# One kernel, two branches: the order of the expert stage written by a list of jobs inside the kernel

## The chip, the cores and the metric

The kernel runs on one core of one Trainium2 chip. The metric is the device time of one execution in microseconds (us). Two kernels are compared by runs that alternate on the same chip; the figure given for a kernel is the median of its runs.

## The reference, cut to what matters

The input x is normalised by rows, and two branches are added to it: a Fourier mixing branch (two DFTs as matrix products) and a branch of 4096 experts that picks, for each of 2048 tokens and 32 heads, two experts and adds their outputs.

```python
x = A_x; xn = layernorm(x)                        # 2048 tokens x 512
out = x + Re(DFT_seq @ (xn @ DFT_hid)) + experts(xn)

def experts(x):                                   # H = 32 heads, K = 2 picks, N = 64 * 64 experts
    q = einsum("nd,dhc->nhc", x, w_q)
    s1, s2 = q[..., :dk] @ k1.T, q[..., dk:] @ k2.T          # 64 scores each
    ...                                           # the two best pairs: gate g, expert number top_e
    act = gelu(einsum("nd,nhkd->nhk", x, u[top_e]))
    return einsum("nhk,nhk,nhkd->nd", g, act, v[top_e])
```

## The kernel before

Up to about 417 us the kernel computes the Fourier branch, the scores and the picks, and prepares the tables u and v as pairs of fp16 parts (high and low, so that each product of two float32 values is three fp16 matmuls). From there on it runs the **expert stage**, which is what the change touches. The picks are not gathered. For each block of 128 tokens (16 blocks, `NT`) the stage computes all 4096 activations and multiplies them by a dense matrix of gates that is zero where nothing was picked. Per block:

- **z products** (`slot`, L1187): x times u for all experts. From block 2 on two blocks form a pair, and a Strassen-like scheme makes 28 slots (`SEQ`, each 24 matmuls of 128 columns) for a pair instead of 32 tile products. A slot writes to one of four PSUM banks ("X", "Y", "Z" of a quad of u tiles; `take` gives a bank, `banks.append` gives it back). Three of the seven operators read sums of u tiles, which are loaded into a ring of three places (`ring_load`, L1170); the first sum is loaded once (`first_sum`, L1132); the sums of x come with `fetch` (L1684, and `prep`, L1090).
- **evictions and gelu** (`z_pair`): ScalarE copies X, Z, X (L1225, L1230, L1232), VectorE adds (L1227, L1235, L1238), ScalarE applies gelu in place (L1215). Some of these free a bank, and slot "4" may start only when the addition after slot "7" (L1238) has read the bank.
- **gates** (`g_prep`): VectorE compares iotas with the list of picks, half a group of 32 tokens at a time: L (L1274), R (L1279), R times gate (L1282). There are three pairs of L and R. `g_mm` (L1290) multiplies them, 32 small matmuls for a group, into one of two PSUM tiles. A block has 4 groups.
- **w** (`w_part`): w1 on VectorE multiplies activations and gates (L1298), w2 on ScalarE casts to fp16 (L1303), w3 on VectorE forms the low part (L1304). All four groups of a block must be done before its v tiles start.
- **v tiles** (`v_tile`, L1352): 16 tiles of 6 matmuls of 512 columns, all into one bank. Seven of the 16 v tables do not fit in SBUF and stream through three places (`v_load`, L1324). `finish` (L1367) adds the result to y, which was loaded (L1361) and had x added by a DMA of GpSimd (L1364); `store` (L1370) writes the block out.
- **checks**: 128 jobs that read the DFT matrices, the weights and the tables again and sum them (`compare`, `compare_in`, `sum_up`, `fit`, `fit_sum`, `fit_here`, the lines with `cx` and `fit`). Nothing in the stage needs them before `verdict`, near the end. They share four buffers.

The order is written by hand in phases: `("z", 0)`, `("z", 1)`, then for each pair b = 2, 4 ... 14 a phase `("a", b)` of 28 slots followed by `("v", b - 1)` of 8 steps, and at the end `("v", 14)` and `("v", 15)`. In phase a the 16 v tiles of block b-2 are put between the slots at fixed places (`TILES`), and two tiles of block b-1 ahead of the last slot; the other 14 tiles of b-1 come in phase v, with no z slot beside them. `put` hangs the gates, w, lists, loads and checks on steps of the phases, and the checks are placed by a clock that counts 2.2 us for a slot and 2.8 us for a v step:

```python
TILES = [1, 2, 3, 3, 4, 6, 8, 10, 11, 13, 15, 17, 18, 20, 22, 24]
for b in PAIRS:
    o, ph, nx = b - 1, ("a", b), ("v", b - 1)
    put(ph, 1, G(o, 0), LRP(o, 1, 0))
    ...
    put(nx, 1, LRP(b, 2, 1), W(b, 0))
    put(nx, 2, W(b, 1))
    put(nx, 3, G(b, 2), LRP(b, 3))
    put(nx, 4, W(b, 2), G(b, 3))
    put(nx, 6, W(b, 3))
```

The framework then lays the instructions out per engine by its own priorities, and derives all semaphores. Only what is passed to `pin` (`keep_in_program_order`) keeps its place: L, the loads and sums of the checks, y loads and stores and the DMA that adds x. Each engine takes its own instructions in the order laid out, and so does SP's queue of DMAs.

Of the kernel before, what the change touches and what calls it, by code (L numbers as in the profile page):

```python
# [18 lines left out]
P = 128  # L19
# [17 lines left out]
def tile_fnet_peer(ctx, tc, x, ca, cb, c5, wt, wf, wr, wq, kt, ut, vn, out):  # L37
# [683 lines left out]
    def part_b(safe, stS, stP, stQ, stE, xt, u_sb, cmp_p, w4):  # L721
# [217 lines left out]
        def compact(b, src, pool, tag):  # L939
# [6 lines left out]
            nc.sync.dma_start_transpose(zt, src)  # L946
            cmp = pool.tile([P, 3, P, 2], F16, tag=tag, name=f"cmp{b}")
            nc.scalar.activation(cmp, zt.unsqueeze(3).to_broadcast([P, 3, P, 2]), AF.Copy)
            CMP[b] = cmp
# [121 lines left out]
        ap0 = stE.enter_context(tc.tile_pool(name="ap0", bufs=1, side="left"))  # L1071
        lr = stE.enter_context(tc.tile_pool(name="lr", bufs=1, side="left"))
# [11 lines left out]
        TG = 32  # L1084
        CB = 4
        ACT = {}

        def prep(b):
            if b > 1:
                nc.sync.dma_start(xb2[:, b % 2].rearrange("p a k n -> p (a k n)"), xt_d[b])  # L1090
# [4 lines left out]
        def u_part(b, cg):  # L1095
# [5 lines left out]
            for cc in range(m):  # L1101
# [4 lines left out]
                for kd in range(KD):  # L1106
                    for l, r in ((0, 0), (0, 1), (1, 0)):
                        nc.tensor.matmul(ps if n == 1 else ps.rearrange("p (b n) -> p b n", b=2),
# [5 lines left out]
            for i, bb in enumerate(b):  # L1114
                nc.scalar.activation(ACT[bb][:, cg * m:cg * m + m, :], pv[:, i], AF.Gelu_apprx_tanh, scale=zsc)

        if not safe:
# [3 lines left out]
            TILES = [1, 2, 3, 3, 4, 6, 8, 10, 11, 13, 15, 17, 18, 20, 22, 24]  # L1121
            TILES0 = [0, 0, 0, 0, 0, 0, 0, 1, 3, 5, 8, 11, 14, 17, 20, 23]
# [7 lines left out]
        def first_sum(qd):  # L1130
            for t, g in enumerate(QUADS[qd]):
                nc.sync.dma_start(u_sb[g][:, :, 1, 0:2, :].rearrange("p l k e -> p l (k e)"),  # L1132
                                  s_d[qd, 0].rearrange("p (t l f) -> t p l f", t=4, l=2)[t])
# [38 lines left out]
        ring_plan()  # L1172
        used = [0]

        def slot(op, quad, bank, qd):

            ua, us, ub, xa = OPS[op]
            for t, g in enumerate(quad):
                k = 0
                for kd in range(2):  # L1180
                    for l, r in ((0, 0), (0, 1), (1, 0)):
# [5 lines left out]
                        nc.tensor.matmul(bank[:, t * P:(t + 1) * P], lt, rt, start=(t == k == 0 and op in "125"),  # L1187
                                         stop=(t == 3 and k == 5), skip_group_check=op not in "125")
                        k += 1
            if us is not None:  # L1190
                ring_load(used[0])
                used[0] += 1

        def z_pair(b, n):

            st = {}
            late = []

            def work(at):

                if True:
                    o = SEQ[at]
                    while late and late[0][0] <= at:
                        late.pop(0)[1]()
                    op, qd = o[0], turn_q(o[1])
                    quad = QUADS[qd]

                    def dst(a, c):
                        return ACT[b[c]][:, 2 * quad[0] + a:2 * quad[3] + 2:2 * (quad[1] - quad[0]), :]

                    def v(p):
                        return p.rearrange("p (t n) -> p t n", t=4)

                    def gelu(d, src=None):
                        nc.scalar.activation(d, d if src is None else src, AF.Gelu_apprx_tanh, scale=zsc)  # L1215

                    def gelu_late(d, n):
                        late.append((at + n, lambda: gelu(d)))

                    if op in "125":  # L1220
                        st[o[1], "X" if op == "1" else "Y" if op == "2" else "Z"] = take(f"z{op}_{b[0]}_{qd}")
                    (X, Xt), (Y, Yt), (Z, Zt) = [st.get((o[1], k), (None, None)) for k in "XYZ"]
                    slot(op, quad, Z if op in "53" else Y if op == "2" else X, qd)
                    if op == "1":
                        nc.scalar.activation(dst(0, 0), v(X), AF.Copy)  # L1225
                    elif op == "2":
                        nc.vector.tensor_tensor(dst(0, 0), v(Y), dst(0, 0), op=ALU.add)  # L1227
                        banks.append(Yt)
                    elif op == "5":
                        nc.scalar.activation(dst(1, 0), v(Z), AF.Copy)  # L1230
                    elif op == "6":
                        nc.scalar.activation(dst(0, 1), v(X), AF.Copy)  # L1232
                        gelu_late(dst(0, 0), 1)
                    elif op == "3":
                        nc.vector.tensor_tensor(dst(0, 1), v(Z), dst(0, 1), op=ALU.add)  # L1235
                        banks.append(Zt)
                    elif op == "7":
                        nc.vector.tensor_tensor(dst(1, 1), v(X), dst(1, 0), op=ALU.add)  # L1238
                        gelu_late(dst(0, 1), 3)
                    else:  # L1240
                        gelu(dst(1, 0), v(X))
                        gelu_late(dst(1, 1), 3)
                        banks.append(Xt)

                    if at + 1 == len(SEQ):
                        while late:
                            late.pop(0)[1]()

            return work

        GP = {}
        pin = tc.keep_in_program_order
# [9 lines left out]
        def g_prep(b, tg, hfs=(0, 1)):  # L1262
            cmp = CMP[b]
            for hf in hfs:
                assert all(k == (b, tg) for k in PREP) and len(PREP.get((b, tg), ())) == hf
                ts = slice(tg * TG + hf * 16, tg * TG + hf * 16 + 16)

                def bc(w, n):
                    return cmp[:, w, ts, :].unsqueeze(2).to_broadcast([P, 16, n // 2, 2])

                LR.append(LR.pop(0))
                L, R = LR[-1]
                PREP.setdefault((b, tg), []).append((L, R))
                pin(nc.vector.tensor_tensor(  # L1274
                    L.rearrange("p t (l two) -> p t l two", two=2),
                    io_lam.rearrange("p (l two) -> p l two", two=2).unsqueeze(1).to_broadcast([P, 16, P // 2, 2]),
                    bc(0, P), op=ALU.is_equal))
                Rv = R.rearrange("p t (c two) -> p t c two", two=2)
                nc.vector.tensor_tensor(  # L1279
                    Rv, io_c.rearrange("p (c two) -> p c two", two=2).unsqueeze(1).to_broadcast([P, 16, NC // 2, 2]),  # L1280
                    bc(1, NC), op=ALU.is_equal)
                nc.vector.tensor_tensor(Rv, Rv, bc(2, NC), op=ALU.mult)  # L1282

        def g_mm(b, tg):
            if (b, tg) not in PREP:
                g_prep(b, tg)
            p = pg(f"g{b}_{tg}")
            for hf, (L, R) in enumerate(PREP.pop((b, tg))):
                for t in range(16):
                    nc.tensor.matmul(p[:, hf, t * NC:(t + 1) * NC], L[:, t, :], R[:, t, :], start=True, stop=True)  # L1290
            GP[b, tg] = p

        def w_part(b, tg, here=False):
            act = ACT[b]
            ts = slice(tg * TG, (tg + 1) * TG)
            p = GP.pop((b, tg))
            w = p.rearrange("p h (n c) -> p c (h n)", c=NC)
            nc.vector.scalar_tensor_tensor(w, act[:, :, ts], fw, w, op0=ALU.mult, op1=ALU.mult)  # L1298
# [611 lines left out]
```

## Time and profile before

| | us |
|---|---|
| three runs: median (lowest, highest) | 1137.82 (1135.99, 1137.84) |
| profiled execution: its time, and its span from first to last instruction | 1138.36, 1136.3 |
| busy in the span: PE, weight loads, VectorE, ScalarE, GpSimd | 1107.2, 722.0, 943.8, 695.9, 332.6 |
| from the first v tile (467.5) to the last matmul (1130.1): PE, VectorE, ScalarE busy | 647.00, 527.03, 356.79 of 662.60 |
| DMA: bytes moved, mean rate over the span | 229.95 MB, 202 GB/s |

PE is TensorE's matmuls, PEld its weight loads, DVE VectorE, ACT ScalarE, POOL GpSimd, SP SyncE; "L1352" is a line of the kernel. Matmuls overlap in the pipeline: a row gives each its full latency, so successive starts tell the rate. The granted clock is 1.00 from 25 us to the last matmul.

### The profile page before, as it was taken

To read this page: it belongs to the slowest core of one execution; us is meant where nothing else is said; L and a number is where in the kernel's file an instruction comes from. 1 tells how busy PE (TensorE), PEld (TensorE's weight loads), DVE (VectorE), ACT (ScalarE), POOL (GpSimd) and SP (SyncE) were. 2 spreads that over 40 slices of the span, in tenths; PEclk is the share of its full clock that TensorE was granted. 3 is DMA by queue.
4 is the path that set the end of the run, shared out by engine and by line. 5 is a ranking of instruction groups with operands and counts; after the bars stand their busy time and mean duration, and the time that the engine had idled before them with its cause. 6 is when DMAs were issued, how large, how long until landed. Compare 5 with 4: busy or idle time off the path is not lost. (4 is left out here: it accounts for less than half of the span.)

```text
span 1136.3 us, 29241 instructions
## 1 busy us (share of the span) xinstructions
PE 1107.2 (97%) x11528; PEld 722.0 (64%) x11528; DVE 943.8 (83%) x2828; ACT 695.9 (61%) x1238; POOL 332.6 (29%) x385
## 2 busy tenths in 40 slices
PE   9999999999999999999999999999999999999997
PEld 6465554544545459787578587587577578578643
DVE  6899789999989799488886976886986986986992
ACT  6557598888877585255566565566556456556530
POOL 0419999898888850000000000000000000000000
PEclk8999999999999999999999999999999999999999
DMA  8884446364353335857776867777676866856644
GB/s 281 272 211 170 159 163 224 112 206 170 101 174 94 112 107 193 158 179 240 254 245 226 275 218 253 251 241 250 216 253 215 301 214 232 283 187 231 178 130 115
DMA packets 134865, 229.95 MB, mean 202 GB/s; under 512 B 35380, under 2 KB 71355, under 8 KB 134718
## 3 DMA queue, kind: packets, MB, share of 16 engines
q1 hardware_dynamic: 132112, 223.72, 60.0%
q0 software_dynamic: 2304, 4.20, 2.4%
q8 instruction: 92, 1.51, 0.5%
q14 instruction: 55, 0.45, 0.1%
q10 hardware_dynamic: 302, 0.08, 0.0%
HBM read 192.49 MB, written 29.69 MB: 196 GB/s over the span
## 5 line engine op out<-in xcount | busy, mean ns | idle before, releaser
L252 PE MATMUL s<-m,xq 128*128 128x512 f16 x1344 | 297.5, 379 | 1.3 <-ACT ss L962 1.3
L1352 PE MATMUL v<-v,act 128*128 128x512 f16 x1044 | 241.4, 379 | 1.1 <-DVE act L1304 0.7
L252 PEld LDWEIGHTS <-xq 128*128 128x128 f16 x1344 | 129.8, 98 | 152.5 <-issue 2.9
L1364 POOL DMA_DIRECT2D y<-in_x_dram x16 | 14.4, 898 | 671.3 <-DMA y<-y_d 327.7
L1187 PEld LDWEIGHTS <-u 128*128 128x128 f16 x2688 | 156.1, 98 | 21.8 <-issue 6.1
L1352 PEld LDWEIGHTS <-act 128*128 128x128 f16 x1044 | 97.2, 98 | 102.7 <-DVE act L1304 1.2
L1274 DVE TENSOR_TENSOR L<-io_lam,cmp 128x2048 f16<-128x2048 f16 x128 | 154.3, 1214 | 4.9 <-PE g L1290 4.9
L966 DVE MAX8 vals<-ss 128x8 f32<-128x64 f32 x896 | 133.5, 217 | 5.4 <-ACT ss L962 5.1
L1187 PEld LDWEIGHTS <-s 128*128 128x128 f16 x1944 | 112.4, 98 | 10.4
L1352 PE MATMUL v<-v,w 128*128 128x512 f16 x480 | 111.1, 379 | 1.4 <-DVE w L1304 0.9
L1303 ACT ACTIVATE act<-g 128x1024 f16<-128x1024 f32 x44 | 57.7, 1311 | 61.8 <-DVE g L1298 61.8
L962 ACT ACTIVATE ss<-s,wsc 128x512 f32<-128x512 f32 x120 | 80.2, 681 | 22.4 <-PE s L252 12.6
L970 DVE FIND_INDEX8 idx<-vals,ss 128x8 uint16<-128x256 f32 x224 | 93.9, 419 | 0.0
L1187 PE MATMUL z<-x,u 128*128 128x128 f16 x1344 | 83.8, 219 | 3.3 <-DVE w L1238 2.9
L1187 PE MATMUL z<-xb,u 128*128 128x128 f16 x1344 | 84.2, 219 | 1.9 <-ACT w L1215 1.8
L1187 PE MATMUL z<-x,s 128*128 128x128 f16 x1296 | 81.1, 219 | 0.0
L1376 ACT ACTIVATE cx<-cx 128x896 f32<-128x896 f32 x68 | 64.1, 942 | 27.7 <-DVE cx L1424 18.1
L1352 PEld LDWEIGHTS <-w 128*128 128x128 f16 x480 | 44.7, 98 | 48.4 <-DVE w L1304 1.4
L1215 ACT ACTIVATE act<-act,scl 128x512 f32<-128x512 f32 x56 | 40.2, 720 | 53.0 <-DVE act L1235 27.9
L1290 PE MATMUL g<-R,L 128*128 128x32 f16 x2048 | 63.1, 176 | 8.6 <-DVE L L1274 5.3
L1290 PEld LDWEIGHTS <-L 128*128 128x128 f16 x2048 | 59.2, 96 | 17.0 <-DVE L L1274 9.4
L1304 DVE TENSOR_TENSOR act<-g,act 128x1024 f16<-128x1024 f32 x44 | 57.3, 1301 | 13.9 <-ACT act L1303 13.5
(358 smaller groups left out, 1884.6 us busy)
## 6 DMA issues: line engine op xcount, KB each, us to landing
s<-s_d SPq DMA_DIRECT2D x81, 512.0 KB, 4.9
v<-v_d SPq DMA_DIRECT2D x67, 512.0 KB, 5.5
cx<-in_cb_dram SPq DMA_DIRECT2D x64, 448.0 KB, 5.5
w<-in_wq_dram SPq DMA_DIRECT2D x28, 512.0 KB, 5.8
fit<-in_wq_dram SPq DMA_DIRECT2D x28, 512.0 KB, 5.1
uv<-in_vn_dram SPq DMA_DIRECT2D x16, 512.0 KB
uv<-in_ut_dram SPq DMA_DIRECT2D x16, 512.0 KB, 3.8
s_d<-v SPq DMA_DIRECT2D x32, 256.0 KB, 2.5
```

The costliest lines, as they stand in the source:

```text
L252: nc.tensor.matmul(ps, xt[i][:, l, kd, :], m[:, r, kd, :], start=(n == 0), stop=(n == 3 * KD - 1))
L962: nc.scalar.activation(s, ps, AF.Copy, scale=inv)
L966: nc.vector.max(vals[:, i, w, :, h], s[:, g, :])
L970: nc.vector.max_index(idx[:, i, w].rearrange("p k h -> p (k h)"), vals[:, i, w, 0:2].rearrange("p k h -> p (k h)"), s[:, w * HC:g + 1, :]. ...
L1187: nc.tensor.matmul(bank[:, t * P:(t + 1) * P], lt, rt, start=(t == k == 0 and op in "125"), stop=(t == 3 and k == 5), skip_group_check=op ...
L1215: nc.scalar.activation(d, d if src is None else src, AF.Gelu_apprx_tanh, scale=zsc)
L1274: pin(nc.vector.tensor_tensor(L.rearrange("p t (l two) -> p t l two", two=2), io_lam.rearrange("p (l two) -> p l two", two=2).unsqueeze(1) ...
L1290: nc.tensor.matmul(p[:, hf, t * NC:(t + 1) * NC], L[:, t, :], R[:, t, :], start=True, stop=True)
L1303: nc.scalar.activation(w16[..., 0], w, AF.Copy)
L1304: nc.vector.tensor_tensor(w16[..., 1], w, w16[..., 0], op=ALU.subtract)
L1352: nc.tensor.matmul(pv, w16[:, c, :, l], v_sb[g][:, r, cc, :], start=(n + cc == 0 and k == 0), stop=(n == end and cc == 1 and k == 2))
L1376: pin(nc.scalar.activation(f, f, AF.Abs, accum_out=chk[:, n:n + 1]))
```

## The change

The phases from `("a", 2)` to `("v", 14)` go, and with them `both`, `fetch`, `TILES` and the table of `put`s (they stay for the fallback branch). In their place a function `stage()` runs while the kernel is built. It makes a list of jobs, each with an engine, a length in ns, what it depends on and a due time: every z slot, v tile, half a group of gate matmuls, every VectorE and ScalarE instruction of the evictions, gates and w, every load, and each step of a check. It then plays the list through: at each moment every free engine takes the ready job with the earliest due time; TensorE takes a ready gate job first, and otherwise the ready head of the z or the v sequence; checks ("fill") are taken when nothing else is ready, or when they are 3 us late. The jobs are issued in the order in which they began, and in the stage all of VectorE, ScalarE and SP and the first matmul of each TensorE job are pinned.

The due times spread the 28 slots of a pair over 24 v tiles (`FULL`) instead of over 16 and two; only the last pair has 18. Gate matmuls go by halves of a group. The arithmetic is the same, and no matmul, eviction or load is added. The parts for blocks 0 and 1 ahead of the stage keep hooks; there the L comparisons are no longer pinned, the preparation of block 1's first gates moves into the stage, and the x part of block 2, its sums and the first ring loads are issued in `("z", 1)`. Block 15's v tiles follow the stage as before.

```diff
+        FULL, LOOK, CHECK0, CHECK1 = (24, 24, 24, 24, 24, 24, 18), 1e9, 12000, 42000
+        LEAD, SOFT, HARD = 8000, 3000, 2000
...
-                nc.sync.dma_start(t.rearrange("p t l k e -> p (t l k e)"), s_d[qd, o])
+                syn.dma_start(t.rearrange("p t l k e -> p (t l k e)"), s_d[qd, o])
...
-            TILES = [1, 2, 3, 3, 4, 6, 8, 10, 11, 13, 15, 17, 18, 20, 22, 24]
...
+            for n, b in enumerate(PAIRS):
+                k = 0
+                for m in range(32):
+                    while k < 28 and m * 28 >= k * FULL[n]:
+                        due["z", n, k] = t
+                        t += 1420
+                        k += 1
+                    due["v", b - 2 + m // 16, m % 16] = t
+                    t += 1450
...
+                    V[b, m] = v = job("PE", 1300, lambda m=m: v_job(b, m), (vload.get((b, g)),), due=due["v", b, m],
+                                      needs="bank" if m == 0 else None)
+                    if b and m == 0:
+                        for w in W2[b]:
+                            v.after(w)
...
+                    z = Z[n, k] = job("PE", 1345, lambda k=k: z_work[n](k), deps, due=at, needs="bank" if op in "125" else None)
...
+                    elif op == "6":
+                        z.after(GE[n, q, "A1"])
+                        ev("A6", "ACT", 600, [z] + region(b + 1, qd), nk("7"))
...
+                    elif op == "7":
+                        z.after(GE[n, q, "A6"])
+                        ev("D7", "DVE", 605, [z, GE[n, q, "A5"]] + region(b + 1, qd), nk("4"))
+                        ev("G11", "ACT", 630, [GE[n, q, "D7"]], at + 12000)
+                    else:
+                        z.after(GE[n, q, "D7"])
+                        ev("G10", "ACT", 600, [z, GE[n, q, "D7"]], at + 3500, "bank")
+                if n + 1 < len(PAIRS):
+                    done = [Z[n, k] for k in range(28)]
+                    for i in range(2):
+                        XF[n + 1, i] = load(done, lambda i=i: prep(b + 2 + i), 256, due["z", n, 27] + 1000)
+                    XF[n + 1, 2] = load(done, lambda: load_x4(b + 2), 512, due["z", n, 27] + 1000)
...
+                start = due["v", b, 0] if ("v", b, 0) in due else total
+                for tg in tgs:
+                    d = start - (4 - tg) * 3400 - 1000
...
+                        old = [halves[i - 3]] if i >= 3 else []
+                        p = job("DVE", 1130, lambda tg=tg, hf=hf: g_prep(b, tg, hf, 0), old + [CM.get(b)], due=d - 4200 + hf * 1700 - LEAD)
+                        p2 = job("DVE", 335, lambda tg=tg, hf=hf: g_prep(b, tg, hf, 1), [p], due=d - 3200 + hf * 1700 - LEAD)
+                        p3 = job("DVE", 335, lambda tg=tg, hf=hf: g_prep(b, tg, hf, 2), [p2], due=d - 2900 + hf * 1700 - LEAD)
+                        g = job("PE", 420, lambda tg=tg, hf=hf: g_mm(b, tg, hf), [p3], due=d - 1800 + hf * 900)
+                        if hf == 0:
+                            if len(WJ) >= 2:
+                                g.after(WJ[-2])
...
+                    w1 = job("DVE", 1200, lambda tg=tg: w_part(b, tg, 0), hf_jobs + gelus(b), due=d)
+                    w2 = job("ACT", 1215, lambda tg=tg: w_part(b, tg, 1), [w1], due=d + 1000)
+                    w3 = job("DVE", 1215, lambda tg=tg: w_part(b, tg, 2), [w2], due=d + 2000)
...
+                crit = [j for j in c if not fill(j)]
+                late = [j for j in c if fill(j) and j.due[1] + SOFT <= now and (e != "SP" or dma[0] < now + 6000)]
...
+            keep_on[0] = True
+            for j in order:
+                keep_first[0] = j.eng == "PE"
+                j.fn()
+            keep_on[0] = False
```

`region(c, qd)` is the list of v tiles of block c-3 that must have read a part of the activation buffer before block c's part is written there: three buffers serve 16 blocks. A job of SP counts 420 ns of its queue (840 for a comparison's two loads, 1250 for the transpose of a list) and 3.1 ns for each KB of its transfer.

More of the change, by code (lines that the diff above doesn't have):

```diff
@@ L1186, in slot @@
                         rt = xb2[:, (0, 0, 1, 1)[xa], r, xa % 2 * 2 + kd, :] if ub is None else x4[:, r, ub, kd, :]
-                        nc.tensor.matmul(bank[:, t * P:(t + 1) * P], lt, rt, start=(t == k == 0 and op in "125"),
+                        mm(bank[:, t * P:(t + 1) * P], lt, rt, start=(t == k == 0 and op in "125"),
                                          stop=(t == 3 and k == 5), skip_group_check=op not in "125")
                         k += 1
-            if us is not None:
-                ring_load(used[0])
-                used[0] += 1
@@ L1194, in z_pair @@
         def z_pair(b, n):
             st = {}
-            late = []
             def work(at):
[L1201 to L1247, printed above, removed]
@@ L1260, in part_b, with g_prep, bc @@
         PREP = {}
-        def g_prep(b, tg, hfs=(0, 1)):
+        def g_prep(b, tg, hf, part):
             cmp = CMP[b]
[L1264 to L1269, printed above, removed]
+            ts = slice(tg * TG + hf * 16, tg * TG + hf * 16 + 16)
+            def bc(w, n):
+                return cmp[:, w, ts, :].unsqueeze(2).to_broadcast([P, 16, n // 2, 2])
+            if part == 0:
@@ L1284, in g_mm @@
[L1284 to L1293, printed above, removed]
+            else:
+                vec.tensor_tensor(Rv, Rv, bc(2, NC), op=ALU.mult)
+        def g_mm(b, tg, hf):
+            if hf == 0:
+                GP[b, tg] = pg(f"g{b}_{tg}")
+            p = GP[b, tg]
+            L, R = PREP.pop((b, tg, hf))
+            for t in range(16):
+                mm(p[:, hf, t * NC:(t + 1) * NC], L[:, t, :], R[:, t, :], start=True, stop=True)
@@ L1351, in v_tile @@
                 for k, (l, r) in enumerate(((0, 0), (0, 1), (1, 0))):
-                    nc.tensor.matmul(pv, w16[:, c, :, l], v_sb[g][:, r, cc, :], start=(n + cc == 0 and k == 0),
+                    mm(pv, w16[:, c, :, l], v_sb[g][:, r, cc, :], start=(n + cc == 0 and k == 0),
                                      stop=(n == end and cc == 1 and k == 2))
-            if g >= V2 and g not in [v for v in v_order(b) if v >= V2][-3:]:
+            if not keep_on[0] and g >= V2 and g not in [v for v in v_order(b) if v >= V2][-3:]:
                 v_load(PL[g])
@@ L1366, in finish @@
         def finish(b, pv):
[L1367 removed]
+            vec.scalar_tensor_tensor(Y[b], pv, osc, Y[b], op0=ALU.mult, op1=ALU.add)
         def store(b):
[L1370 removed]
+            (syn.dma_start(out[b * P:(b + 1) * P], Y[b]))
         T = {}
@@ L1731, in part_b, with __init__, after @@
-        begun = None
-        for n, ph in enumerate(phases):
+        for b in range(NT):
+            ACT[b] = act_tile(b)
+        class Job:
+            def __init__(self, eng, ns, fn, deps=(), due=None, tail=None, size=0, needs=None, frees=None):
+                self.eng, self.ns, self.fn, self.due, self.size = eng, ns, fn, due, size
+                self.tail = dict(PE=225, DVE=145, ACT=155, SP=0, POOL=6000)[eng] if tail is None else tail
+                self.needs, self.frees = needs, frees
+                self.users, self.left, self.ready, self.done = [], 0, 0, None
+                for d in deps:
+                    if d is not None:
+                        self.after(d)
+            def after(self, d):
+                d.users.append(self)
+                self.left += 1
@@ L1733, in part_b @@
+        for ph in phases:
             b = ph[1]
             if ph[0] == "z":
-                ACT[b] = act_tile(b)
                 for cg in range(8):
@@ L1738, in part_b @@
                     hooks(ph, cg)
+                if b and not safe:
+                    stage()
                 continue
             if ph[0] == "a":
-                begun = both(b)
+                if safe:
+                    for c in (b, b + 1):
+                        prep(c)
+                    for n in range(16):
+                        v_job(b - 2, n)
+                    end_v(b - 2)
+                    for k in range(28):
+                        if k * 16 // 28 != (k - 1) * 16 // 28:
+                            u_part((b, b + 1), k * 16 // 28)
+                        hooks(ph, k)
                 continue
-            pv, pvt = begun or take(f"v{b}")
+            if b < 15 and not safe:
+                continue
+            VB[b] = take(f"v{b}")
             for cg in range(8):
-                if begun is None or cg:
-                    v_part(b, pv, cg)
+                v_part(b, VB[b][0], cg)
                 hooks(ph, cg)
-                if cg == 1 and b % 2 and b < 13:
-                    fetch(b + 3)
                 if b + 1 == NT and cg == 3 and not safe:
```

643 lines of the change are left out of this document (455 added, 188 removed).

## The prediction

> **What bounds the kernel now.** I read the page's busy shares first, then the stage's busy time by window, alone and by source line, then the waits of TensorE, then the timeline of one crossing from a pair's last z slot to the next block's v tiles, and last the waits of VectorE and the DMA queue. The stage from its first v tile to its last matmul, whole and for the matmuls of z (L1187), v (L1352) and gates (L1290) alone:
>
> ```profile
> span 1136.3 us, 29241 instructions
> ...
> 467.50:1130.10 662.60, 647.00 (x8175) 461.89 (x8172) 527.03 (x896) 356.79 (x660) 14.41 (x17) 1.00 0.69 226
> ...
> 467.50:1130.10 662.60, 286.19 (x4704) 272.65 (x4704) 1.00 0.69 226
> ...
> 467.50:1130.10 662.60, 352.33 (x1524) 141.86 (x1524) 1.00 0.69 226
> ...
> 467.50:1130.10 662.60, 59.29 (x1920) 55.66 (x1920) 1.00 0.69 226
> ```
>
> TensorE is busy 647.0 of 662.6 us, VectorE 527 (80%), ScalarE 357 (54%). The busy time counts each matmul's whole latency, so the true room is found from starts. This is TensorE alone in the timeline, around the end of one pair:
>
> ```profile
> 709.91 1.50 PE L1187 MATMUL z<-x,u 128*128 128x128 f16 x24
> 711.25 7.93 PE L1352 MATMUL v<-v,w 128*128 128x512 f16 x36
> 719.02 0.95 PE L1290 MATMUL g<-R,L 128*128 128x32 f16 x32
> 719.83 2.75 PE L1352 MATMUL v<-v,w 128*128 128x512 f16 x12
> 722.41 0.55 PE L1290 MATMUL g<-R,L 128*128 128x32 f16 x16
> 723.93 0.55 PE L1290 MATMUL g<-R,L 128*128 128x32 f16 x16 [0.97 <-DVE R L1282]
> 724.34 7.93 PE L1352 MATMUL v<-v,w 128*128 128x512 f16 x36
> 732.10 1.50 PE L1187 MATMUL z<-xb,u 128*128 128x128 f16 x24
> 733.44 1.46 PE L1352 MATMUL v<-v,act 128*128 128x512 f16 x6
> ```
>
> A z slot takes 711.25 - 709.91 = 1.34 us (0.0558 a matmul), 36 v matmuls 7.77 (0.2157 each, 1.29 a tile), 32 gate matmuls 0.81 (0.0253 each). So the stage's matmuls without any gap need 4704 x 0.0558 = 262.5, 1524 x 0.2157 = 328.7, 1920 x 0.0253 = 48.6 and the 24 half-width ones of the last tiles (L1337) 24 x 0.108 = 2.6, together 642.4. The stage has 662.6: **TensorE loses 20.2 us in the stage**, and no reordering can win more. Who makes it wait:
>
> ```profile
> PE g L1290 <- DVE L L1274: 4.6, 8, 1.3
> PE g L1290 <- DVE R L1282: 3.2, 4, 1.0
> PE z L1187 <- DVE w L1238: 2.9, 3, 1.8
> PE z L1187 <- ACT w L1215: 1.8, 2, 1.3
> PE v L1352 <- DVE w L1304: 0.9, 1, 0.9
> ```
>
> These five groups are 13.4 us in 18 waits: 7.8 for gates placed ahead of their L and R, 4.7 for z slots whose bank or addition is late, 0.9 for the w of the next block. Each wait is counted from the modelled end of the matmul before it, so it is short by 0.16 (a v matmul lasts 1.46 - 5 x 0.2157 = 0.38, the next may start after 0.22); this and small waits make up the rest. No engine is full, and the waits are spread out: an order that is a little wrong in many places, which is what the change rewrites.
>
> **The change part by part.** No instruction is removed, so the sum is 1138.36 (the profiled execution; 0.54 above the median) minus 20.2 plus what TensorE still waits for.
>
> *Gates, 7.8 now.* A half group is issued when the list holds its L and R for ready. It is as good as the lengths in the list, and the trace has these:
>
> ```profile
> 712.24 2.48 DVE L1298 SCALAR_TENSOR_TENSOR g<-act,scl,g 128x1024 f32<-128x1024 f32 x2
> ...
> 718.28 0.94 DVE L1418 TENSOR_TENSOR cx<-cx 128x768 f32<-128x768 f32 x1
> ...
> 720.80 1.22 DVE L1274 TENSOR_TENSOR L<-io_lam,cmp 128x2048 f16<-128x2048 f16 x1
> ...
> 728.52 1.22 DVE L1274 TENSOR_TENSOR L<-io_lam,cmp 128x2048 f16<-128x2048 f16 x1
> 729.65 1.29 DVE L1304 TENSOR_TENSOR act<-g,act 128x1024 f16<-128x1024 f32 x1
> ```
>
> L to the next start takes 729.65 - 728.52 = 1.13 (list 1.13); two w1 take 2.48 with the tail of the last, about 1.20 each (list 1.20); w3 follows with 1.29, tail included (list 1.215 plus 0.145). The order should hold on the chip. But TensorE's gate job has no slack beyond the rest of the job before it, on average half of 1.3 us, so a VectorE that is late by more shows again. I keep 2.5 of 7.8 (bounds 0 and 7.8).
>
> *Evictions, 4.7 now.* In the list a z slot that waits for its addition lets v tiles pass, where before the tiles stood at fixed places. I keep 1.5 (bounds 0 and 4.7).
>
> *w at the end, 0.9 in the five groups.* The last pair keeps its 18 tiles, so the tail has the same shape, with the checks ended 42 us ahead of the list's end and VectorE freer. I keep 0.5. The waits that the groups do not hold, 20.2 - 13.4 = 6.8, shrink in the same ratio, (2.5 + 1.5 + 0.5) / 13.4 = 0.34: 2.3.
>
> *24 tiles instead of 18 beside the slots.* This adds a risk. The v tiles of the even block need all four of its w, which need the gelu of the pair's last slot. In the rows above the last slot starts at 709.91; 36 + 12 + 36 v matmuls (14 tiles) and two gates cover 711.25 to 732.10; the last w3 ends at 729.65 + 1.29 = 730.94, **19.7 us after the z end**. After the change 8 tiles are left: 8 x 1.29 = 10.3, two gates 1.6, and then five slots of the next pair (1a 5a 2a 6a 3a) that need nothing of that block, 6.7: 18.6 us. Slot 7a must wait for an eviction that overwrites the buffer the block's first four v tiles read. So the chain of 19.7 has to get shorter by 1.1 or TensorE stands still at each of six crossings. It should: between 717 and 731 VectorE also made two L that block does not need yet (2.3 with 720.80 and 728.52, of which one is for its last half) and comparisons (0.94 and smaller ones), and the third gate stood behind 36 v matmuls until 719.02 though its predecessors' w3 had ended. By due times I count from the z end: gelu 1, two w1 2.4, one hand-over to ScalarE and back 1.5, two w3 2.4, one L with its R 1.8, two w1 and two w3 4.8, one more hand-over 1.5, together 15.4. That is 3.2 inside the cover; a comparison that is already running (up to 0.9) and the additions of the next slots (two or three of 0.6) eat most of it. I take 0.5 at each of six crossings, 3.0 (bounds 0 and (19.7 - 18.6 + 2.3) x 6 = 20, where the chain stays as it is and the next slots' additions come on top).
>
> *Loads and SP's queue.* All loads move; their number stays. Rows: issues, KB each and us to landing; then the line of the x load with its issue time in ns, and its time to landing.
>
> ```profile
> s<-s_d SPq DMA_DIRECT2D x81, 512.0 KB, 4.9
> v<-v_d SPq DMA_DIRECT2D x67, 512.0 KB, 5.5
> ...
> L1090 SPq DMA_DIRECT2D xb<-xt_d x14: 326/420/490, 446.4 to 982.0; - x14
> ...
> DMA to landing us min/median/max: 3.5/4.1/4.9
> ```
>
> The next pair's x (two loads and one of 512 KB) is issued at the z end instead of some us later, and is needed 10 to 12 us after it: three issues of 0.42 plus 4.9 is 6.2, hidden by the eight tiles. If the queue has 5 us of checks ahead, it is 11, just in time. Ring loads wait for a slot's end, v loads for a tile's end, stores for `finish`; all stand in one queue, so a late matmul holds up the loads behind it, and DVE's checks behind those. SP has the room: 148 issues in the two big rows are 62 us of 662. The 16 loads of first sums count as four jobs of 0.42 in the list and cost 1.7 each; slot 5a waits for four of them, issued after block 3's x at the end of block 1's z products: 0.4 + 1.7 + 4.1 = 6.2 us, covered by slot 1a and four v tiles (6.5). I add 0.3 for this start and 0.3 for transfers. POOL's job (adding x to y) only moves with the y loads, and `finish` is not due until 20 us later: nothing. The blocks before the stage keep their order but for the unpinned L: nothing, bounds -1 and +1.
>
> Sum: 2.5 + 1.5 + 0.5 + 2.3 + 3.0 + 0.3 + 0.3 = 10.4. 1138.36 - 20.2 + 10.4 = 1128.6, against the median 0.54 less: **1128 us**.
>
> **The rivals.**
>
> (1) *The plan holds almost wholly.* The list lets every engine take what is ready, and VectorE has 20% to spare. Gate, z and w waits 1 us, crossings 0, rest 1, transfers 0.6: 1137.8 - 20.2 + 2.6 = 1120. For it: the lengths agree to 2%. Against: each gate stands without slack, and transfers aren't constant (3.5 to 4.9 in the rows above).
>
> (2) *Buffers make the waits, not the order.* Three L/R pairs, two gate tiles and four banks stay as they are. If they hold VectorE back, the list meets the same walls: 1137.8 minus a tail of 0.9, 1137. What VectorE waited for:
>
> ```profile
> DVE R L1279 <- PE g L1290: 17.9, 4, 14.8
> ...
> DVE L L1274 <- PE g L1290: 1.9, 3, 0.9
> ```
>
> VectorE waited 1.9 us for a free L, three times, and once very long for a free R (14.8 of 17.9, one place). TensorE's 12 waits for L and R are not behind these. [...]
>
> (3) *Slower: the crossing runs dry.* With eight tiles left instead of 14, TensorE waits for w six times. If the chain stays 19.7 us and the next slots' additions lengthen it to 22, that is 3.4 each, 20 in all instead of 3: 1128 + 17 = 1145. For it: the row of 1.29 that ends at 730.94, against a cover of 18.6. Against: the comparisons and the early L in between, which due times put back. It decides from (20.2 - 7.4) / 6 = 2.1 us at each crossing, a chain of 20.7.
>
> **How the numbers follow.** My forecast (1123 to 1134) 0.52; the plan holds almost wholly (under 1123) 0.16; buffers, or waits that come back elsewhere (1134 to 1140) 0.16; the dry crossing (over 1140, or 1136 to 1140 in a milder form) 0.16. A change within 0.2% (2.3 us) cannot be told from none. Faster by more, under 1135.5: 0.52 + 0.16 and a third of the third case, 0.74; same 0.09; slower 0.17. The range that leaves out no more than 2 in 10 is 1118 (2 us above the stage without any wait, 1137.8 - 20.2 = 1117.6, rounded) to 1139; the likeliest case's own is 1123 to 1134.
>
> **What would show it.** Right: the stage of TensorE shrinks to about 652 us with 4704, 1524 and 1920 matmuls in it; waits of gates for L and R under 3 us; z slots waiting for L1238's and L1215's successors under 2; after each z end eight v tiles, then slots of the next pair, and the last w3 within 16 us. Wrong: waits of v tiles for w3 at every crossing (rival 3); VectorE waiting for gates before L or R (rival 2); loads landing late ahead of z slots or checks holding up VectorE; or a z slot waiting for x in the first 12 us of a pair.

## The result, and the profile after

| | before | after |
|---|---|---|
| median of the runs, lowest to highest (us) | 1137.83, 1135.99 to 1138.03 | 1116.94, 1116.67 to 1117.59 |
| profiled execution: time, span (us) | 1138.36, 1136.3 | 1117.59, 1115.7 |

The ratio is 0.9821 with a 95% interval of 0.9804 to 0.9838: **20.9 us faster**. I had forecast 1128 us, so the sign was right and the gain less than half of what came. Rival 1 happened, and a little more than it.

In the kernel after, nearly all instructions of the stage are issued through two wrappers and show their lines: L1098 for VectorE, ScalarE and SP, L1103 for TensorE. So operations are told apart by tile names (z, v, g, w, act, L, R, cx).

First the busy time by window, with the prediction's columns (window, its length, then busy time and instructions of PE, PEld, DVE, ACT, POOL, granted clock, DMA share, GB/s). Before, the last 50 us ahead of the stage:

```profile
417.50:467.50 50.00, 47.99 (x905) 46.78 (x904) 42.82 (x122) 27.27 (x34) 6.71 (x4) 1.00 0.66 160
```

After, the same 50 us, then the stage from its own first v tile (465.8) to the last matmul (1108.6), and the end:

```profile
417.50:467.50 50.00, 50.00 (x934) 48.60 (x932) 41.75 (x117) 27.51 (x35) 6.09 (x4) 1.00 0.40 129
465.80:1108.60 642.80, 641.78 (x8152) 460.63 (x8149) 521.12 (x897) 356.67 (x660) 14.21 (x17) 1.00 0.70 235
1108.60:1115.70 7.10, 0.01 (x1) 0.00 (x0) 0.48 (x1) 0.00 (x0) 0.00 (x0) 0.87 0.14 44
```

From the first v tile to the last matmul it took 662.60 us and takes 642.80; 1.34 of the difference is the first z slot of the first pair, which now runs ahead of the first v tile. VectorE and ScalarE do what they did (521.12 and 356.67 us, 527.03 and 356.79 before): the same work, placed otherwise. TensorE is busy 641.78 of 642.80. The 50 us ahead of the stage were part of the gain too: 47.99 us busy before, 50.00 after. The end behind the last matmul is 7.10 us, 0.9 longer than before. TensorE's waits from 417 us on, all that the trace names, after (engine and tile, released by; us in total, times, longest):

```profile
PE v L1103 <- DVE act L1098: 0.7, 1, 0.7
PE g L1103 <- DVE R L1098: 0.3, 1, 0.3
```

Counted from starts (each matmul's start less the one before and the step of its size), TensorE lost 22.4 us from 417 us on before, 20.0 of them in the stage and 2.3 ahead of it, and 1.7 after. 22.4 - 1.7 = 20.7, less the 0.9 at the end, is 19.8 of the 20.6 us between the two spans; another 0.6 is that the first z product starts at 418.4 instead of 419.1.

The 2.3 us are two places in the z products of blocks 0 and 1. TensorE's timeline there (start, us, engine, line, operation, count, in brackets the idle time before), before:

```profile
457.14 0.96 PE L1290 MATMUL g<-R,L 128*128 128x32 f16 x32 [0.69 <-DVE L L1274]
457.96 3.79 PE L1108 MATMUL z<-xb,u 128*128 128x128 f16 x65
463.06 2.13 PE L1108 MATMUL z<-xb,u 128*128 128x128 f16 x35 [1.32 <-issue]
```

and after:

```profile
455.67 0.95 PE L1103 MATMUL g<-R,L 128*128 128x32 f16 x32
456.47 8.70 PE L1103 MATMUL z<-xb,u 128*128 128x128 f16 x153
```

Neither the gate's wait for L nor the hole ahead of 463.06 is there any more.

Now the crossing that the prediction showed, from a pair's last z slot (start 707.31) to the first v tile of the even block (725.97), TensorE after:

```profile
707.31 1.50 PE L1103 MATMUL z<-x,u 128*128 128x128 f16 x24
708.65 5.34 PE L1103 MATMUL v<-v,w 128*128 128x512 f16 x24
713.83 0.55 PE L1103 MATMUL g<-R,L 128*128 128x32 f16 x16
714.23 1.46 PE L1103 MATMUL v<-v,w 128*128 128x512 f16 x6
715.52 0.95 PE L1103 MATMUL g<-R,L 128*128 128x32 f16 x32
716.33 2.75 PE L1103 MATMUL v<-v,w 128*128 128x512 f16 x12
718.91 0.55 PE L1103 MATMUL g<-R,L 128*128 128x32 f16 x16
719.32 1.46 PE L1103 MATMUL v<-v,w 128*128 128x512 f16 x6
720.61 1.50 PE L1103 MATMUL z<-xb,u 128*128 128x128 f16 x24
721.95 1.50 PE L1103 MATMUL z<-x,u 128*128 128x128 f16 x24
723.29 1.50 PE L1103 MATMUL z<-xb,u 128*128 128x128 f16 x24
724.63 1.50 PE L1103 MATMUL z<-x,s 128*128 128x128 f16 x24
725.97 2.75 PE L1103 MATMUL v<-v,act 128*128 128x512 f16 x12
```

No row has idle time before it. Eight v tiles (24 + 6 + 12 + 6 matmuls), four half groups of gates and four slots of the next pair lie between, as the list was to do it. VectorE in the second half of that stretch, where the last two groups of w are made:

```profile
717.67 0.95 DVE L1098 TENSOR_TENSOR cx<-cx 128x768 f32<-128x768 f32 x1
718.54 1.22 DVE L1098 TENSOR_TENSOR L<-io_lam,cmp 128x2048 f16<-128x2048 f16 x1
719.67 1.28 DVE L1098 TENSOR_TENSOR act<-g,act 128x1024 f16<-128x1024 f32 x1
720.86 1.26 DVE L1098 SCALAR_TENSOR_TENSOR g<-act,scl,g 128x1024 f32<-128x1024 f32 x1
...
724.38 1.30 DVE L1098 TENSOR_TENSOR act<-g,act 128x1024 f16<-128x1024 f32 x1
```

The last w3 ends at 725.68, 17.0 us after the z end at 708.65, and the v tile that needs it starts 0.29 us later. Checks (cx) and an L still stand inside the chain: the chain is not packed on VectorE, and it is just in time all the same.

### The profile page after: what moved, and what is told of

Read it like the earlier page. It is cut to its first block, busy times and chain, and to the rows that moved or that the text cites. A ratio compares the mean times of both kernels' runs of the same rounds, so it can differ in the third digit from the quotient of the medians.

```text
span 1115.7 us, 29227 instructions
## 1 busy us (share of the span) xinstructions
PE 1102.7 (99%) x11528; PEld 721.8 (65%) x11528; DVE 937.7 (84%) x2828; ACT 695.8 (62%) x1238; POOL 333.4 (30%) x385
## 4 chain that ended last, share of the span: by engine, by line
PE 80%; DVE 7%; POOL 6%; DMA 3%; ACT 2%; issue 1%; SPq 0%; POOLq 0%; ACTq 0%; DVEq 0%
PE z L1103 27%; PE v L1103 27%; PE s L252 19%; PE g L1103 4%; PE m L148 1%; POOL v L795 1%; DVE L L1098 1%; DVE vals L972 1%; PE m L152 1%; PE p L449 1%; DVE idx L976 1%; DVE g L1098 1%; DMA xt_d<-xq 1%; POOL u L540 1%; POOL v L825 1%
## 5 line engine op out<-in xcount | busy, mean ns | idle before, releaser
L1103 PE MATMUL v<-v,act 128*128 128x512 f16 (+1 forms) x1068 | 248.3, 377 | 0.7 <-DVE act L1098 0.7
L1103 PEld LDWEIGHTS <-u 128*128 128x128 f16 x3456 | 198.3, 98 | 14.4
L1103 PEld LDWEIGHTS <-act 128*128 128x128 f16 x1068 | 97.9, 98 | 95.7 <-DVE act L1098 1.2
L1098 DVE TENSOR_TENSOR L<-io_lam,cmp 128x2048 f16<-128x2048 f16 x120 | 144.9, 1220 | 6.9 <-PE g L1103 6.7
L1103 PE MATMUL z<-xb,u 128*128 128x128 f16 x2112 | 127.7, 219 | 0.0
L1103 PEld LDWEIGHTS <-s 128*128 128x128 f16 x1944 | 113.4, 98 | 12.5
L1103 PE MATMUL v<-v,w 128*128 128x512 f16 x480 | 113.0, 379 | 0.0
L1098 ACT ACTIVATE cx<-cx 128x896 f32<-128x896 f32 (+2 forms) x134 | 83.5, 625 | 31.7 <-DVE cx L1098 30.3
L968 ACT ACTIVATE ss<-s,wsc 128x512 f32<-128x512 f32 x120 | 80.1, 680 | 22.4 <-PE s L252 12.6
L1098 DVE TENSOR_TENSOR cx<-cx 128x128 f32<-128x128 f32 (+9 forms) x226 | 91.7, 418 | 2.7 <-DMA cx<-in_cb_dram 1.1
L1103 PE MATMUL z<-x,u 128*128 128x128 f16 x1344 | 84.2, 219 | 0.0
L1098 ACT ACTIVATE act<-act,scl 128x512 f32<-128x512 f32 x56 | 40.2, 719 | 66.4 <-DVE act L1098 66.4
L1103 PE MATMUL z<-x,s 128*128 128x128 f16 x1296 | 81.2, 219 | 0.0
L1103 PEld LDWEIGHTS <-L 128*128 128x128 f16 x2048 | 65.0, 96 | 16.1 <-DVE R L1098 0.7
L1098 ACT ACTIVATE act<-g 128x1024 f16<-128x1024 f32 x40 | 51.5, 1311 | 37.3 <-DVE g L1098 36.9
L1098 DVE TENSOR_TENSOR act<-z,act 128x512 f32<-128x512 f32 x44 | 30.4, 690 | 49.7 <-PE z L1103 45.9
L1103 PEld LDWEIGHTS <-w 128*128 128x128 f16 x480 | 43.8, 98 | 43.2
```

What stands on the lines that cost most here:

```text
L968: nc.scalar.activation(s, ps, AF.Copy, scale=inv)
L1098: return (lambda *a, **k: pin(f(*a, **k))) if keep_on[0] else f
L1103: i = nc.tensor.matmul(*a, **k)
```

## The experiments

Each run is told as its ratio to the kernel before on the same chip, with the 95% interval, and its median. "After" stands at 0.9821. "Lost" is TensorE's loss from the stage's start on, counted from starts as above.

### Is it the order as issued, or the pins?

**e_nopin**: the list's order of issue, nothing in it pinned.

```diff
-                return (lambda *a, **k: pin(f(*a, **k))) if keep_on[0] else f
+                return f
...
-            if keep_on[0] and keep_first[0]:
+            if False:
```

> The changed kernel with nothing pinned: jobs are issued in the list's order, TensorE's order stays the same to the instruction, and the framework lays out VectorE, ScalarE and SP by its own priorities. Theory A (the gain is the order in which VectorE, ScalarE and SP take their work): waits of gates and z slots come back, 8 to 18 us of the 20, so 1125 to 1135 us. Theory B (the gain is where v tiles and z slots stand on TensorE): nothing is lost, 1117 to 1119 us.

Measured 1.0311 (1.0275 to 1.0348), 1171.18 us. TensorE took its jobs in the same order as after. VectorE's waits, and then TensorE's:

```profile
DVE cx L1442 <- DMA cx<-in_cb_dram: 38.9, 14, 8.3
```

```profile
PE z L1103 <- DVE act L1265: 13.2, 11, 2.9
PE g L1103 <- DVE R L1304: 11.0, 6, 6.1
```

In the stage VectorE stood 38.9 us at checks whose data had not landed, with the additions and gates that TensorE needed queued behind. TensorE lost 40.3 us in the stage, and 13.3 ahead of its first v tile, where VectorE took a check of the stage among the gates of block 1:

```profile
457.87 0.43 DVE L1426 TENSOR_TENSOR cx<-cx 128x256 f32<-128x256 f32 x1 [10.07 <-DMA fit<-in_wq_dram]
```

Without its pins the change would have been 34 us slower than the kernel before (1171.18 against 1136.85 on that chip).

**b_pin**: the kernel before with its hand-written order pinned on all engines through the same wrappers.

```diff
+        vec, sca, syn = Kept(nc.vector), Kept(nc.scalar), Kept(nc.sync)
...
+            keep_on[0] = not safe and ph[0] != "z" and ph != ("v", 15)
```

> The kernel before with its order by hand, but every instruction of VectorE, ScalarE and SP and the first matmul of each job pinned in that order from the first pair on. If the hand's order is what makes TensorE wait: no gain, 1135 to 1150 us (the framework's own shifts had even helped). If the framework's layout spoils a good order: 1120 to 1130 us.

Measured 1.0853 (1.0813 to 1.0892), 1232.71 us; the first of TensorE's waits:

```profile
PE g L1096 <- DVE R L1091: 49.5, 30, 3.2
```

Pins alone are no gain either: the hand order was only a sketch, and the framework's rearrangement was worth 96 us to it (1232.71 against 1136.85). It takes the list's order and the pins together.

**e_pindve** and **e_pindveact**: the list's order, with only VectorE pinned, and with VectorE and ScalarE pinned and SP's queue left free (TensorE's first matmuls pinned in both).

```diff
-                return (lambda *a, **k: pin(f(*a, **k))) if keep_on[0] else f
+                return (lambda *a, **k: pin(f(*a, **k))) if keep_on[0] and self.eng is nc.vector else f
```

(for the second, `self.eng is not nc.sync`).

> The changed kernel with VectorE alone pinned in the list's order (and TensorE, whose order stays the same in any case); the framework lays out ScalarE and SP. All unpinned took 1171 us. If VectorE's order carries the gain: 1117 to 1122 us. If the order of SP's loads does (VectorE's comparisons waited 39 us for loads when nothing was pinned): 1135 to 1170 us.

> VectorE, ScalarE and TensorE keep the list's order, SP's queue is left to the framework. With VectorE alone pinned the time was 1149.6 us, with 73 us of ScalarE waiting for tables of the checks (24 waits) and evictions queued behind. Theory A (it was ScalarE's own order that put the checks ahead of evictions): under 1122 us, ScalarE's waits for loads of checks under 15 us, TensorE's waits under 5. Theory B (it was SP's order that brought the loads late, whatever ScalarE's order): 1135 to 1155, with ScalarE still waiting over 50 us for loads. Between them (1122 to 1135) both queues matter.

Measured 1.0104 (1.0077 to 1.0132), 1149.57 us, and 0.9826 (0.9798 to 0.9854), 1117.51 us. ScalarE's longest wait in the first:

```profile
ACT fit L1551 <- DMA fit<-in_wq_dram: 73.2, 24, 6.3
```

With ScalarE free, sums of the checks were laid ahead of evictions and waited 73.2 us for their tables, and VectorE and then TensorE waited for the evictions. With ScalarE pinned as well that row is gone, and TensorE has the same two waits as after (0.7 and 0.3 us). So SP's own order carries nothing that can be measured; of what the pins carry, the two engines' order carries all.

### What made TensorE wait before?

**b_nochecks**: the kernel before without its 128 check jobs; `verdict` fills its flags with zeros.

```diff
-            for m, job in enumerate(jobs):
+            for m, job in enumerate(()):
```

> The kernel before without its 128 checks and without the verdict's arithmetic (that part of the computation is left out; the result does not need it). If the comparisons that stand between gates and w are what TensorE waits for: 1120 to 1126 us. If the order of gates, w and evictions among themselves is: 1131 to 1137 us.

Measured 0.9823 (0.9778 to 0.9868), 1118.17 us. The stage from its first v tile to its last matmul, and TensorE's waits:

```profile
464.30:1110.30 646.00, 644.17 (x8176) 461.95 (x8173) 429.40 (x573) 213.49 (x270) 12.95 (x15) 1.00 0.48 151
```

```profile
PE g L1290 <- DVE R L1282: 1.1, 1, 1.1
PE z L1187 <- DVE act L1238: 0.3, 1, 0.3
```

Within the interval, the kernel before without the checks is as fast as the kernel after with them. Counted from starts, TensorE loses 3.4 us in the stage instead of 20.0. So the checks made 17 of the 20 us: 98 us of VectorE and 143 of ScalarE (527.03 - 429.40 and 356.79 - 213.49), engines which had room, but the checks stood in the queues ahead of what TensorE needed. Their loads go too (DMA share 0.48 instead of 0.69), but after has a share of 0.70 and hardly a wait, so it isn't the traffic. It need not be the checks' busy time alone: before, VectorE also stood 23.1 us at checks whose loads had not landed, against 1.1 us after, and this run takes both away together.

```profile
DVE cx L1418 <- DMA cx<-in_cb_dram: 12.9, 7, 4.7
DVE cx L1407 <- DMA cx<-in_cb_dram: 6.2, 4, 3.0
DVE cx L1405 <- DMA cx<-in_cb_dram: 4.0, 2, 2.4
...
DVE cx L1098 <- DMA cx<-in_cb_dram: 1.1, 2, 0.9
```

(The last row is after's.) VectorE's timeline before, at the prediction's crossing, shows one place where a check stood in the way:

```profile
718.28 0.94 DVE L1418 TENSOR_TENSOR cx<-cx 128x768 f32<-128x768 f32 x1
719.26 0.29 DVE L1424 TENSOR_TENSOR cx<-cx 128x126 f32<-128x126 f32 x1
...
719.66 1.22 DVE L1274 TENSOR_TENSOR L<-io_lam,cmp 128x2048 f16<-128x2048 f16 x1
...
723.46 0.42 DVE L1282 TENSOR_TENSOR R<-R,cmp 128x512 f16<-128x512 f16 x1
```

1.38 us of a check's sums (718.28 to 719.66) stand ahead of the L and R that end at 723.88; the gates start at 723.93, after the 0.97 us of idle time that the prediction quoted. Not tried: the hand order with the checks alone placed by lengths; so it is open whether the list's order of the other work adds anything of its own; the 3.4 us left here against 1.7 after leave little room for it.

**e_checkdue**: checks compete with all other jobs by due time once that is reached, instead of coming second.

```diff
+                c = [j for j in c if not fill(j) or j.due[1] <= now]
+                j = min(c, key=lambda j: j.due[1] if fill(j) else j.due)
```

> The changed kernel with the checks no longer second: from their due time on they compete with gates, evictions and w by due time alone, on VectorE, ScalarE and SP. If the rank of the checks carries the gain: gates and w come late behind comparisons, 1122 to 1132 us. If it does not: 1117 to 1119 us.

Measured 0.9811 (0.9775 to 0.9847), 1118.58 us. Lost: 4.6 us instead of 1.7, within the intervals. So the rank of the checks carries nothing that can be measured, as long as the list places them too.

### What do the 24 tiles carry, and where does the crossing run dry?

**e_full18**, **e_full28**: 18 and 28 v tiles beside a pair's 28 slots instead of 24. **e_strict**: TensorE may take only the earlier due of the two heads.

```diff
-        FULL, LOOK, CHECK0, CHECK1 = (24, 24, 24, 24, 24, 24, 18), 1e9, 12000, 42000
+        FULL, LOOK, CHECK0, CHECK1 = (18, 18, 18, 18, 18, 18, 18), 1e9, 12000, 42000    # e_full18
+        FULL, LOOK, CHECK0, CHECK1 = (28, 28, 28, 28, 28, 28, 18), 1e9, 12000, 42000    # e_full28
+        FULL, LOOK, CHECK0, CHECK1 = (24, 24, 24, 24, 24, 24, 18), 1e-9, 12000, 42000   # e_strict
```

> The changed kernel with the slots of every pair spread over 18 tiles instead of 24, as many as before the change. Theory A: the list keeps everything busy anyway, 1117 to 1119 us. Theory B (the spread over 24 tiles carries a part): evictions get 0.4 us less per slot, z waits come back, 1121 to 1127 us.

> The changed kernel with the slots of the first six pairs spread over 28 tiles instead of 24, so that four tiles of the odd block are left at the z end instead of eight. By the prediction's crossing the cover is then 4 x 1.29 + 1.6 + 6.7 = 13.5 us against a chain of 15.4 (its count) to 18 us (the changed kernel's last w3): TensorE stands 2 to 4.5 us at each of six crossings, 1129 to 1144 us. If the list finds other work there: 1117 to 1120 us.

> The changed kernel with LOOK near 0: in the list TensorE may take only the head with the earliest due time, so a z slot no longer passes a v tile that waits, nor a tile a slot. The v tiles of the even block are due 8 tiles and one slot after the z end (10.3 + 1.3 + gates 1.6 = 13.2 us), while their last w3 ended 15.9 to 18.2 us after it in the changed kernel. Theory B: TensorE stands 3 to 5 us at each of six crossings, 1135 to 1147 us. Theory A: VectorE brings the w forward as soon as TensorE waits for it (15.4 us by the prediction's count), 2 us at each, about 1130 us.

Measured: 18 tiles 0.9814 (0.9786 to 0.9843), 1116.36 us; 28 tiles 0.9929 (0.9908 to 0.9951), 1131.76 us; strict 1.0023 (1.0007 to 1.0039), 1140.30 us. So the 24 tiles bring nothing. TensorE's waits from 467 us on with 28 tiles:

```profile
PE v L1103 <- DVE act L1098: 4.5, 3, 1.6
PE g L1103 <- DVE R L1098: 3.1, 3, 2.4
PE v L1103 <- ACT w L1098: 1.9, 1, 1.9
```

These are, the second apart, the waits of v tiles for w2 and w3 that rival 3 named. With five tiles and five slots between, the first v tile is taken 14.8 to 17.8 us after the z end, while the last w3 ends 15.4 to 18.5 us after it: later at each of the six crossings. In e_strict only one slot of the next pair got ahead of the even block's tiles, and v tiles and gates stood 2.2 to 3.5 us at each crossing. So with 24 tiles it is the slots that pass the tiles which hold the crossing together; the chain is about as long as with 28.

### How true must the lengths be?

**e_dve80, e_dve90, e_dve95, e_dve110**: every VectorE length in the list times 0.8, 0.9, 0.95 and 1.1; the program computes the same, in another order.

```diff
-                self.eng, self.ns, self.fn, self.due, self.size = eng, ns, fn, due, size
+                self.eng, self.ns, self.fn, self.due, self.size = eng, ns * (0.8 if eng == "DVE" else 1), fn, due, size
```

> The changed kernel with VectorE's lengths in the list 20% too short, so the list believes L, R, w1 and w3 ready before they are. The prediction's step (a gate or slot is placed without slack, and each lateness shows): 5 to 15 us of waits, 1122 to 1132 us. The other theory (VectorE waits for TensorE every few us, 73 us in all in the changed kernel, so lateness is paid back there and cannot add up): under 3 us, 1117 to 1120 us.

> The changed kernel with VectorE's lengths in the list 5% too short. 20% too short cost 58 us. If the loss goes with the error from the start (the prediction's step, no slack anywhere): a quarter, 10 to 15 us, 1127 to 1132 us. If the gates' slack (median 1.3 us in the changed kernel) takes up a small error: under 3 us, 1117 to 1120 us.

> The changed kernel with VectorE's lengths in the list 10% too long. Gates and slots are then never early on the chip, but the list may run out of VectorE's time (it believes 86% instead of 78%) and put w and gates late. If only lateness against the list costs: 1117 to 1119 us. If the list's own room counts: 1122 to 1130 us.

> All VectorE lengths in the list times 0.9. So far: 1.10 gave 1118.8, 1.00 gave 1117, 0.95 gave 1128.5, 0.80 gave 1176.6 us. If lateness grows in proportion to the error (theory A, some 2.3 us for each 1%): 1138 to 1145. If it grows slowly first and then steeply, where VectorE as listed is more than full (theory B): 1129 to 1136. Waits of gates for R over 6 us in both.

| VectorE's lengths | ratio (95%) | median us | lost us |
|---|---|---|---|
| x 1.10 | 0.9836 (0.9811 to 0.9861) | 1118.81 | 2.6 |
| x 1.00 (after) | 0.9821 (0.9804 to 0.9838) | 1116.94 | 1.7 |
| x 0.95 | 0.9914 (0.9889 to 0.9939) | 1128.46 | 14.6 |
| x 0.90 | 1.0048 (1.0026 to 1.0070) | 1142.83 | 28.6 |
| x 0.80 | 1.0326 (1.0284 to 1.0368) | 1176.61 | 58.8 |

TensorE's largest group of waits at 0.80:

```profile
PE g L1103 <- DVE R L1098: 24.6, 28, 2.1
```

The ratios give (0.9914 - 0.9821) x 1137.8 = 10.6 us for the first 5%, 15.2 for the next, 31.6 for the next 10%: two to three us for each 1%, and nothing on the long side. Half the gain is gone at 5%, all of it at 10%. The proportional curve had the time at 0.90 right, though its slope grows a little.

### The two places ahead of the stage

**e_pinl**: L of blocks 0 and 1 pinned again, as it was before.

```diff
-                vec.tensor_tensor(
+                i = vec.tensor_tensor(
...
-                    bc(0, P), op=ALU.is_equal)
+                    bc(0, P), op=ALU.is_equal); i = keep_on[0] or pin(i)
```

> The changed kernel with L pinned again in the blocks ahead of the stage, as before the change. Two waits of 2.3 us in all stood there before and are gone. If the pin made them: 1119 us with both back near 456 and 461 us. If the moves of the preparation and loads did: 1117 us, none back.

Measured 0.9819 (0.9795 to 0.9843), 1117.95 us. In the trace the gate's wait for L at 456 us is back (0.7 us), the hole at 463 is not. So the pin made the first; 0.7 us is under what the times can tell. What made the second isn't shown. ScalarE before stood there at the cast of a list whose transpose had not landed, with an eviction of a z bank behind it (461.69), and after has no such cast from 424.5 us to 473.5:

```profile
460.94 0.84 ACT L948 ACTIVATE cmp<-zt 128x768 f16<-128x768 f16 x1 [5.76 <-DMA zt<-z_d]
```

## Why the prediction was wrong in size

**The floor** was right for the stage: no gap can be won twice. My 642.4 for the matmuls alone is 641.1 without the slot that went ahead of the first v tile, and the stage took 642.8. **Blocks ahead of the stage** I put at "nothing, bounds -1 and +1": measured -2.3. The row of 47.99 busy us in 50.00 was there to be read, and I asked only the stage for its waits. That is also why the time lies below the low end of my range. I called 1118 "2 us above the stage without any wait", but 1137.8 - 20.2 is the stage without any wait itself, with nothing for what lies ahead of it.

**What TensorE still waits for** is the step that failed. I kept 10.4 us; the trace has 1.7 in the stage.

| term | kept | measured after |
|---|---|---|
| gates | 2.5 | 0.4 (one wait) |
| evictions | 1.5 | 0 |
| w at the end | 0.5 | 0.9 (one wait) |
| waits that no group holds, by the ratio 0.34 | 2.3 | 0.4 |
| crossings | 3.0 | 0 |
| start and transfers | 0.6 | 0 |

- *Gates.* "TensorE's gate job has no slack ... so a VectorE that is late by more shows again" is right as a mechanism: at 0.95 TensorE loses, counted from starts, 9.1 us in 35 places ahead of gates, 5.0 ahead of v tiles and 0.7 ahead of z slots. That the whole then comes to 1128, my very forecast, is chance: my sum had other terms. But I had no row for a late VectorE. My rows said the contrary: L 1.13 against 1.13 in the list, w1 1.20 against 1.20, w3 1.145 against 1.215. I kept 10.4 us, about what lengths 5% too short cost (10.6), in a list whose lengths I had just found true. On the chip half of the gates start within 1.32 us after their R ends (the median of 120; 8.7 before), and the trace names one wait. Little slack is what a plan that holds looks like.
- *Evictions* and the *ratio* go with it: I scaled waits whose maker I had not looked for. It was mostly the checks (b_nochecks: 17 of 20 us), and the list, whose lengths are true, takes the waits away almost wholly, not in part.
- *Crossings.* I counted a chain of 15.4 us; it is 15.9 to 18.2. The L at 718.54 and the cx at 717.67 inside it are about 2 us that I had left out of the count and put into the 3.2 of room. The cover of 18.6 was right: the v tiles start 16.0 to 18.7 us after the z end. So the chain nearly fills the cover, and stalls are zero, where I took 0.5 for each. TensorE's choice between v head and z head makes that (e_strict): a slot more is taken when w is late (five at one crossing, four at the others). I had counted five slots into the cover, and still kept 0.5 for a chain that runs over it; it never did (18.2 at most against 18.6).
- *Start, loads and SP's queue*: nothing to see, as I had it but for 0.6; e_pindveact shows SP's order free.

**The rivals.** Rival 1, with 2.6 kept, has 1.7 in the trace; 1138.4 - 20.2 + 1.7 - 2.3 ahead of the stage - 0.6 ahead of the z products + 0.9 at the end is 1117.9, against 1117.6 for the profiled execution. Its chance of 0.16 was too low: the rows of lengths spoke for it and I gave more weight to "each gate stands without slack". Rival 2 (buffers) is out: b_nochecks has the same buffers and banks, and TensorE loses 3.4 us, though VectorE itself waits 50.8 us there for a free L or R (1.9 and 17.9 before). TensorE's gaps before were mostly made by work standing in a queue: 17 of the 20 us went with the checks. Rival 3 (a dry crossing) is real and was one step away: 28 tiles bring it. Of the signs I named, the eight tiles followed by slots are there (seven once), gate waits are under 3, no z slot waits; "w3 within 16 us" was wrong (17.0 in the crossing shown), and the stage came to 642.8 instead of 652.

## What to carry to other kernels

Filler work on an engine with room still costs time when it stands ahead of what the full engine needs next (17 of the 20 us here): find the maker of a wait (here by leaving the checks out) before deciding how much of the wait will stay. An order planned in the program works when the engines that carry the chain keep it (by the ratios, without pins 56 us were lost, 13 of them ahead of the stage, and with VectorE alone pinned 32), when the full engine may pass a blocked head (23 us), and when lengths are true or long (5% short cost 11 us, 10% long nothing). So for a forecast compare the plan's lengths with the trace: where they agree, expect the plan to hold.

## What the runs showed of the hardware

With 28 tiles a dry crossing cost more than its wait. TensorE in that run, in two places, and the windows around them and around a third, with the granted clock (1.00 is full speed) in the third column from the end:

```profile
559.45 0.61 PE L1103 MATMUL v<-v,w 128*128 128x512 f16 x2 [1.91 <-ACT w L1098]
560.98 5.31 PE L1103 MATMUL v<-v,w 128*128 128x512 f16 x16 [0.92 <-DVE w L1098]
...
738.37 0.56 PE L1103 MATMUL g<-R,L 128*128 128x32 f16 x16 [2.41 <-DVE R L1098]
738.78 5.54 PE L1103 MATMUL v<-v,act 128*128 128x512 f16 x17
```

```profile
558.00:561.40 3.40, 1.03 (x4) 0.33 (x5) 3.40 (x8) 2.90 (x4) 0.00 (x0) 1.00 0.87 298
561.40:564.80 3.40, 3.40 (x9) 1.22 (x8) 3.40 (x11) 1.54 (x5) 0.86 (x1) 0.50 0.61 206
564.80:568.20 3.40, 3.40 (x44) 1.95 (x43) 3.06 (x6) 1.78 (x6) 0.00 (x0) 1.00 0.88 233
...
646.70:650.10 3.40, 1.68 (x22) 1.01 (x19) 3.40 (x5) 2.83 (x4) 0.86 (x1) 1.00 0.73 171
650.10:653.50 3.40, 2.68 (x27) 1.50 (x28) 3.40 (x8) 2.62 (x10) 0.00 (x0) 1.00 1.00 231
...
738.90:742.30 3.40, 3.40 (x11) 1.04 (x8) 3.40 (x6) 3.40 (x10) 0.00 (x0) 0.50 0.86 318
```

Two pauses of 1.91 and 0.92 us, with two matmuls between, were followed by a granted clock of 0.50 in the window from 561.40 to 564.80; in the next window it was 1.00 again. The 16 v matmuls from 560.98 took 5.31 us, as long as 24 at the clock of 1.00 in the kernel after (5.34 from 708.65). A single pause of 2.41 us was followed by 0.50 in the window from 738.90 to 742.30. How long TensorE stood does not decide it alone: it was busy 1.68 and 2.68 of 3.40 us in the two windows from 646.70, so it stood 2.44 us there in all, and the clock was 1.00 in both. What decides it is not shown.

With v matmuls 0.2157 us apart and 0.38 for the last one, as the prediction read them, the 16 would have taken 3.62 us and the 17 from 738.78 3.83: by this estimate the lower clock added 1.7 us at each of the two places. Over longer stretches the mean granted clock was 0.99 in e_strict (467.50 to 1100.00) and 0.96 in b_pin (467.50 to 1222.00); what that added to their times is not measured. In the kernels before and after it was 1.00 in each 10 us from 415 to 1125 and to 1105. I had priced rival 3 at the waits alone, which is too low.
